# Other block borders for the routing, a limit on its steps, and a later tile: local-global attention and a mixture of experts on one core

## The chip, the core and the metric

The kernel runs on one core of one Trainium2 chip. Its time is device time in microseconds (us) of one execution. Of the kernel before three runs were taken, and the median counts. One more execution was recorded by the hardware profiler.

## The reference

Four batches of 8 heads, 768 tokens of 64 values each, go through an attention in which a token sees the 8 first tokens and the last 96 up to itself, with a bias that grows with the distance. The outputs, 3072 tokens of 512 values, go through a layer of 8 experts, of which each token takes the two with the highest noisy logits. Cut to its core:

```python
scores = scale * np.matmul(q, k.transpose(0, 1, 3, 2)) - slopes * dist      # kept where global or local
a = np.exp(scores - max); a = a / (sum(a) + 1e-9)
x = (a @ v).transpose(0, 2, 1, 3).reshape(3072, 512)

logits = x @ w_gate                                        # 3072 x 8
noisy = logits + np.log1p(np.exp(x @ w_noise)) * noise
top2 = the two largest of noisy in each row                # expert numbers
w = softmax over these two
for e in range(8):
    for k in range(2):
        m = top2[:, k] == e
        out[m] += w[m, k] * (np.maximum(x[m] @ w1[e], 0) @ w2[e])   # w1: 512x1024, w2: 1024x512
```

## The kernel before

**Tiles and stages.** The tokens are 24 tiles of 128. The first stage, the attention, ends a little after 155 us in the trace (its last L899); expert 0 follows, and then the other seven experts, in an order that the kernel finds itself. All of it is one program with an order written out by hand: each engine does its instructions in the order in which the Python code issues them. Multiplications of float32 data in the experts are made of three of a shorter type each: `cut` (lines 195 to 197) has ScalarE round a tensor to its high part (L196) and VectorE subtract that from it (L197).

**Half blocks.** The attention loop (its body is in `tile_local_global_attention_then_moe`, the `for n in range(0, NPAIR, 2)`) goes over half blocks, two to a tile, four heads each. In one of them come, in this order: `score` for the half block after it (L862 on VectorE, four instructions), `trans` (L878, transposes on TensorE), for the tile before `gate_s` or `gate_t`, `product` for the second next (L848 on TensorE), `norm` for the half block before the last (L910, L912, L915 on VectorE; its result `y` is a tile of x), `attend` (L899 on TensorE), `gate_s` or `gate_l`, and `finish`. So a tile's attention and its gate (`gate_t`: transposes; `gate_l`: logits, L410; `gate_s`: a selector product, L423 or L426) lie some half blocks apart. The gate products are made for two tiles at once; `partner` says which go together, and the last tile of a block with an odd number of tiles (`ALONE`) has one for itself, L410, with its transposed tile in `ys[2]`.

**Routing.** The tiles fall into five blocks (`SEG`), of 6, 6, 5, 4 and 3 tiles. When the last tile of a block has its logits, a generator `route(r)` does the block's routing: the noise's softplus (L472 to L497), the two largest (`max` L502, `max_index` L504), positions of the tokens in their expert by TensorE (L552, L554), and then per tile a `mask` (L579), a `marks` (L603, 128 x 336 values on VectorE) and, per up to three tiles (all in the third block), a table sum on TensorE (L628) that L632 adds to a table `tab` of token numbers and weights. The table thus tells for each expert and place which token stands there. Only one block at a time may be in its marks (`marking`). Block 2 (`CLOSE`), the third, closes the tokens from which expert 0's first 512 are taken: it gathers them at once, from the copy `xe` that `gate_l` stores of every tile up to the block's end (`xe<-y` in the trace). Blocks 3 and 4 give the rest.

A generator does its next step when the loop calls it: `tick(place)` after each of the four scores and each of the three steps of a norm lets one active generator do one step, and `finish` lets each do up to 5 (3 for the first two blocks) more. A generator that waits for another engine says so and is passed over until a later place.

**Expert 0 and what runs beside it.** The first four tiles of tokens are transposed (`turn`), and then `up(0, f)` for f = 0 to 7 makes 12 matmuls of 512 columns each (L1132), evicted by `evict` (ScalarE L1113, VectorE L1117). After each third matmul `ahead()` works off one of 32 slots of a table `slots`: it takes the fourth block's generator (`late`) or the fifth's (`last`) up to a step whose number stands there. When all 96 are done `rank()` orders the experts by their counts (from L290 on VectorE), and GpSimd gathers expert 0's last 300 tokens, while TensorE does `down` (L1169). `whole_words` (L236, GpSimd copies) puts their words together, `turn` (L347, in banks named `sc` too) transposes them, and the second half of expert 0's first layer (`up(1, f)`) and of its second (`second(0)`) follow. While `second(0)` runs, `prepare(1)` lists what makes expert 1's operands ready: `weights` (cuts of w1's blocks, `w1_`) and `tokens` (four parts a tile: sums, L1319 to L1322, and three cuts; `z` is the last tile, of 22 tokens a half). The first product of expert 1 is L1426, in a bank named `bank`. From there on the order is the same in both kernels.

The two lists that the change and the prediction speak of most:

```python
SEG = [(0, 6), (6, 12), (12, 17), (17, 21), (21, NT)]              # line 66
...
x, y, z = (tokens(1, t) for t in range(1, 4))
return [*pair[2:], x[0], *join[4:6], w1_[0], *x[1:3], join[6], x[3], *held[:2], y[0], held[2], *y[1:3],
        *w1_[1:], y[3], *z[:3], *get[:2], z[3]]                    # prepare(1), line 1345
```

## Time and profile before

| | us |
|---|---|
| runs | 697.83, 699.15, 701.33 |
| median | 699.15 |
| profiled execution, its own time | 698.98 |
| span of its instructions | 697.3 |
| mean granted TensorE clock | 0.998 |

The profile's page gives the busy time of each engine over the span. Two of its lines matter beside those shown further down: the memory system moved 116.61 MB at a mean of 167 GB/s, and the granted clock of TensorE stood at 9 (90% or more) in each of the 40 slices of the span. A row of the timeline stands for one or more instructions of one line in direct succession: its start, the time from the start of the first to the end of the last, engine, line, operation, output and inputs by the program's names with their shapes, the count, and in brackets, where the engine was idle just before, for how long and what it had waited for. The end of a matmul is modelled, so that rows of TensorE overlap; its starts are measured.

### The profile page before, as it was taken

The numbers are of one execution on the slowest core, as the hardware profiler recorded it, in microseconds if no ns is written. First come the engines' busy times: TensorE is split into PE (matmuls) and PEld (weight loads), VectorE is DVE, ScalarE is ACT, GpSimd is POOL, SyncE is SP. The second block draws the span as 40 slices with busy tenths as digits, with TensorE's granted clock in tenths as the row PEclk, the third lists the DMA queues.
The fourth block names the chain that finished last, engine by engine and source line by source line (L and its number), as shares of the span: only waits on it lengthen the run. The fifth ranks groups of instructions, "written<-read, shape, count | busy, mean of one in ns | idle before, by whom it ended". The sixth has DMA issues, their size and how long they took to land. (4 is left out here: it accounts for less than half of the span.)

```text
span 697.3 us, 16022 instructions
## 1 busy us (share of the span) xinstructions
PE 682.5 (98%) x5701; PEld 615.8 (88%) x5701; DVE 460.2 (66%) x1412; ACT 424.3 (61%) x912; POOL 325.6 (47%) x408
## 2 busy tenths in 40 slices
PE   7999999999999999999999999999999999999995
PEld 5888888888889899999999998999998899889984
DVE  6668788968938478557846694767367757847500
ACT  6888787762346576557755774585458547745510
POOL 3352738350188672264536445552745344541222
PEclk9999999999999999999999999999999999999999
DMA  8999988859394898267945874695569547943233
GB/s 240 331 300 312 275 250 264 305 181 334 128 273 88 155 199 159 52 120 163 193 69 116 183 157 79 140 189 110 93 151 240 94 107 165 186 72 91 31 47 49
DMA packets 132889, 116.61 MB, mean 167 GB/s; under 512 B 51866, under 2 KB 97050, under 8 KB 132800
## 3 DMA queue, kind: packets, MB, share of 16 engines
q1 hardware_dynamic: 121392, 89.35, 46.8%
q0 software_dynamic: 11264, 25.89, 21.4%
q8 instruction: 47, 0.77, 0.5%
q10 hardware_dynamic: 144, 0.26, 0.2%
q14 instruction: 42, 0.34, 0.1%
HBM read 71.07 MB, written 33.10 MB: 149 GB/s over the span
## 5 line engine op out<-in xcount | busy, mean ns | idle before, releaser
L1426 PE MATMUL bank<-xh,wall 128*128 128x384 f32 (+4 forms) x784 | 216.1, 342 | 0.0
L1426 PEld LDWEIGHTS bank<-xh,wall 128*128 128x128 f32 x784 | 144.1, 188 | 3.2
L1426 PE MATMUL bank<-xl,wall 128*128 128x384 f32 (+4 forms) x392 | 133.5, 341 | 1.4 <-DVE xl L197 1.4
L1145 POOL DMA_INDIRECT out_dram<-y,ids x40 | 65.1, 1628 | 123.8 <-ACT y L1142 120.9
L1169 PE MATMUL av<-w2h,hh 128*128 128x512 f32 x304 | 119.6, 393 | 0.0
L1169 PE MATMUL av<-w2h,hl 128*128 128x512 f32 x304 | 119.1, 392 | 0.0
L1169 PE MATMUL av<-w2l,hh 128*128 128x512 f32 x304 | 119.1, 392 | 0.0
L197 DVE TENSOR_TENSOR wall<-raw,wall 128x512 fp32r<-128x512 f32 (+1 forms) x84 | 76.0, 912 | 52.9 <-ACT wall L196 52.9
L196 ACT ACTIVATE wall<-raw 128x512 fp32r<-128x512 f32 (+1 forms) x84 | 57.9, 699 | 45.6 <-POOL raw L1279 45.5
L1117 DVE SCALAR_TENSOR_TENSOR hl<-bank,hh 128x384 fp32r<-128x384 f32 (+4 forms) x84 | 47.2, 562 | 51.0 <-ACT hh L1113 50.5
L1426 PEld LDWEIGHTS bank<-xl,wall 128*128 128x128 f32 x392 | 73.9, 188 | 4.5 <-DVE xl L197 1.8
L865 ACT ACTIVATE a<-ns,mx 128x168 f32<-128x168 f32 (+1 forms) x192 | 67.9, 423 | 14.6 <-DVE mx L862 14.2
L251 POOL DMA_INDIRECT xg<-xd,ids x49 | 53.1, 1084 | 41.6 <-DVE place L302 29.8
L862 DVE CUSTOM_DVE_ANT_0 ns<-sc,bias 128x168 f32<-128x168 f32 (+1 forms) x188 | 51.9, 321 | 25.0 <-PE sc L848 11.4
L1169 PEld LDWEIGHTS av<-w2h,hl 128*128 128x128 f32 x304 | 57.1, 188 | 12.6
L1169 PEld LDWEIGHTS av<-w2l,hh 128*128 128x128 f32 x304 | 57.1, 188 | 9.3 <-DVE w2l L197 0.3
L1169 PEld LDWEIGHTS av<-w2h,hh 128*128 128x128 f32 x304 | 57.1, 188 | 9.1
L1113 ACT ACTIVATE hh<-bank 128x384 fp32r<-128x384 f32 (+4 forms) x84 | 41.8, 498 | 37.0 <-DVE bank L1500 24.7
L1278 POOL TENSOR_TENSOR raw<-raw 128x256 f32<-128x256 f32 x28 | 22.5, 803 | 81.4 <-DVE wall L197 80.8
L899 PE MATMUL av<-vs,at 128*64 128x65 f32 (+1 forms) x768 | 57.3, 224 | 0.0
L236 POOL COPY xt<-y 128x256 uint16<-128x256 uint16 x96 | 35.1, 403 | 46.4 <-DVE y L915 43.6
L899 PEld LDWEIGHTS av<-vs,at 128*64 128x64 f32 (+1 forms) x768 | 50.8, 136 | 2.4 <-issue 1.8
(219 smaller groups left out, 1466.1 us busy)
## 6 DMA issues: line engine op xcount, KB each, us to landing
raw<-in_w SPq DMA_DIRECT2D x64, 256.0 KB
raw<-in_w SPq DMA_DIRECT2D x32, 512.0 KB
out_dram<-zero SPq DMA_DIRECT2D x14, 512.0 KB
vs<-in_v SPq DMA_DIRECT2D x24, 260.0 KB
xd<-xt SPq DMA_DIRECT2D x24, 256.0 KB
qbuf<-in_q SPq DMA_DIRECT2D x23, 256.0 KB
ks<-in_k SPq DMA_DIRECT2D x20, 272.0 KB
xe<-y SPq DMA_DIRECT2D x17, 256.0 KB
```

Source lines behind the costliest of these rows:

```text
L196: nc.scalar.activation(hi, src, AF.Copy)
L197: eng.tensor_sub(lo, src, hi.bitcast(F32))
L236: nc.gpsimd.tensor_copy(to[:, :, c], frm[:, :, c])
L251: nc.gpsimd.indirect_dma_start(out=xg[e, t].bitcast(U16)[:m], out_offset=None, in_=xd[:n], in_offset=bass.IndirectOffsetOnAxis(ap=r, axis= ...
L862: nc.vector.tensor_tensor_reduce(out=ns[x][:, s, :w], in0=ps[:, s], in1=bias[:, u + x, s] if i else bias0[:, u + x, s], scale=-scale, scal ...
L865: nc.scalar.activation(A[n + x][:, s * w:(s + 1) * w], ns[x][:, s, :w], AF.Exp, bias=mx[x][:, s:s + 1], scale=-1.0)
L899: nc.tensor.matmul(ps[s * Q:(s + 1) * Q, h], a[r:z, part * P + q0:part * P + q0 + Q], t[r:z, c], start=k == 0 and (n == 1 or h == 0), stop ...
L1113: nc.scalar.activation(inner(e)[0][j][:, f, :src.shape[1]], src, AF.Relu)
L1117: nc.vector.scalar_tensor_tensor(lo, src, 0.0, hi.bitcast(F32), op0=OP.max, op1=OP.subtract)
L1145: ins = nc.gpsimd.indirect_dma_start(out=out, out_offset=bass.IndirectOffsetOnAxis(ap=r, axis=0), in_=y, in_offset=None, bounds_check=N + ...
L1169: nc.tensor.matmul(ps, x[j][:, f, cols], w[:, f], start=n == 0, stop=n == 3 * FC - 1)
L1426: nc.tensor.matmul(ps, wb[c % 2][u][:, 2 * a + k], x[v][:, 2 * b + k], start=start and n == 0, stop=stop and n == 5, skip_group_check=True)
```

## The change

- The blocks are 6, 6, 4, 4 and 4 tiles. No tile is alone in its gate product any more; `ys[2]` is not used for it, and the last pair's transposed tiles stand in two tiles of their own (`xg`), where they stood in `pairs[0]`. Tile 16 belongs to the fourth block, so it isn't stored in `xe`.
- A generator's steps in one half block are limited by `PACE`: to 10 when the third block's routing is active, to 6 when the fourth's (or the fifth's) is; the other blocks' have no limit. The count `left` is shared by `tick` and `finish`.
- The addition of 2.0 in the softplus (L476) is made by ScalarE, and the step that stood for it remains only in the last two blocks. The copy of token numbers into `val` goes away, since `val` is one tile for all blocks, into which the numbers are written once at the start.
- The table `slots` is timed anew. Before, `late` was asked for its end in slot 29 and `last` stood at step 52 in slot 31; now `late` is asked for its end in slot 17, and `last` stands at step 63 in slot 31.
- In `prepare(1)`, `w1_[1:]`, the last two cuts of weights, move from before `y[3]` (the third tile's last cut) to the list's end; the parts of the last tile `z` and two gathers for the expert after it (`get`) stand in another order.

```diff
-    SEG = [(0, 6), (6, 12), (12, 17), (17, 21), (21, NT)]
+    SEG = [(0, 6), (6, 12), (12, 16), (16, 20), (20, NT)]
...
-    tok = consts.tile([P, NT, 2], F32, name="tok")
+    vals = small.tile([P, NT, 2, 3], F32, name="val")
...
-            if j == 0:
-                XT[g + 1] = pairs[0].rearrange("p (k j t) -> p k j t", k=KC, j=2)
-            to = XT[g + 1 - j][:, :, j]
+            if j == 0 and g == NT - 2:
+                XT[g + 1] = [gp.tile([P, Dm], F32, name="xg", bufs=7).rearrange("p (k t) -> p k t", k=KC) for _ in "ab"]
+            elif j == 0:
+                x = pairs[0].rearrange("p (k j t) -> p k j t", k=KC, j=2)
+                XT[g + 1] = [x[:, :, i] for i in range(2)]
+            to = XT[g + 1 - j][j]
...
         nc.scalar.activation(u, u, AF.Exp, scale=-1.0)
+        nc.scalar.activation(t, u, AF.Copy, bias=2.0)
         yield True
-        nc.vector.tensor_scalar(t, u, 2.0, None, op0=OP.add)
-        yield
+        if r > CLOSE:
+            yield
         nc.vector.reciprocal(t, t)
...
-        val = small.tile([P, SW, 2, 3], F32, name="val")[:, :w]
+        val = vals[:, a:z]
...
-            nc.vector.tensor_copy(val[:, :, :, 0], tok[:, a:z])
...
+        PACE = (99,99,10,6,6)
+        left = [0]
+
         def begin():
+            left[0] = min([PACE[r] for _, r in active], default=99)
...
         def go(y):
             x = y[0]
+            left[0] -= 1
...
-                if y[0].ready <= place:
+                if y[0].ready <= place and left[0] > 0:
                     return go(y)
...
-                while n and y in active and y[0].ready <= END:
+                while n and y in active and y[0].ready <= END and left[0] > 0:
...
-            28: [(last, 48)], 29: [(late, 99), split], 30: [split], 31: [(last, 52)],
+            28: [(last, 57)], 29: [split], 30: [(last, 61), split], 31: [(last, 63)],
...
-                        *w1_[1:], y[3], *z[:3], *get[:2], z[3]]
+                        get[0], y[3], *z[:2], get[1], z[3], z[2], *w1_[1:]]
```

Three places show how instructions move. In the lists an instruction stands with its line, operation, output and inputs, with the elements of one partition behind the 128; "x2" is two in succession. Lines of the changed kernel are 3 to 8 higher than those of the one before.

**VectorE, the norm behind the tile of y whose place a store still reads**, at 115.50 us in the trace (the tile is written by L915, in the change L923). L502 and L504 (L506 and L508) are the third block's two largest, L603 (L606) the marks of the second block, L862 (L870) the scores. Before:

```order
L915 TENSOR_TENSOR y_98<-av,den 128x256
L502 MAX aside<-aside 128x8
L504 MAX_INDEX aside<-aside 128x8
L502 MAX aside<-aside 128x8
L504 MAX_INDEX aside<-aside 128x8
L502 MAX aside<-aside 128x8
L504 MAX_INDEX aside<-aside 128x8
L502 MAX aside<-aside 128x8
L504 MAX_INDEX aside<-aside 128x8 x2
L508 TENSOR_TENSOR aside<-aside 128x5
L510 CAST ixf_3042<-aside 128x10
```

and after the change:

```order
L923 TENSOR_TENSOR y_98<-av,den 128x256
L506 MAX aside<-aside 128x8
L508 MAX_INDEX aside<-aside 128x8
L606 TENSOR_TENSOR xg<-aside 128x336 x2
L870 ISA ns,mx<-sc,bias 128x168
L870 ISA mx 128x1
L506 MAX aside<-aside 128x8
L508 MAX_INDEX aside<-aside 128x8
L870 ISA ns,mx<-sc,bias 128x168
L870 ISA mx 128x1
L506 MAX aside<-aside 128x8
L508 MAX_INDEX aside<-aside 128x8
```

What came in one row behind such a norm is now spread between the scores of the next half block, and the second block's marks, which were past by then, stand ahead of these scores.

**TensorE, the end of the up products of expert 0** (L1132, in the change L1140; `at` and `sc` are the banks of the seventh and the eighth product, `lg` that of the table sums, L628 and L631). Before:

```order
L628 MATMUL lg<-xg,wall 128x168 x2
L1132 MATMUL at<-wall,xh 128x512 x2
L1132 MATMUL at<-wall,xl 128x512
L1132 MATMUL sc<-wall,xh 128x512 x2
L1132 MATMUL sc<-wall,xl 128x512
...
L1132 MATMUL sc<-wall,xh 128x512 x2
L1132 MATMUL sc<-wall,xl 128x512
L628 MATMUL lg<-xg,wall 128x168 x6
```

and after:

```order
L631 MATMUL lg<-xg,wall 128x168 x6
L1140 MATMUL at<-wall,xh 128x512 x2
L1140 MATMUL at<-wall,xl 128x512
L1140 MATMUL sc<-wall,xh 128x512 x2
L1140 MATMUL sc<-wall,xl 128x512
...
L1140 MATMUL sc<-wall,xh 128x512 x2
L1140 MATMUL sc<-wall,xl 128x512
L631 MATMUL lg<-xg,wall 128x168 x2
L1140 MATMUL sc<-wall,xh 128x512 x2
L1140 MATMUL sc<-wall,xl 128x512
```

The first row before is the fourth block's last sum. The sum over the three tiles of the last block (six matmuls) stood behind the eighth product; now the sum over its first three tiles stands fifteen matmuls before that product's end, and the one over its fourth tile nine matmuls behind the seventh product.

**VectorE, ahead of the first product of expert 1.** `xl` and `wall` are the low parts of tokens and weights, 128x44 the sums of the 22-token tile. Before:

```order
L197 TENSOR_TENSOR xl<-xg,xh 128x2x128
L197 TENSOR_TENSOR wall<-raw,wall 128x768
L197 TENSOR_TENSOR wall<-raw,wall 128x512
L197 TENSOR_TENSOR xl<-aside,xh 128x8x128
L1319 TENSOR_TENSOR aside<-xg 128x44
...
L1322 TENSOR_TENSOR aside<-aside,xg 128x44
L197 TENSOR_TENSOR xl<-xg,xh 128x4x22
L197 TENSOR_TENSOR xl<-xg,xh 128x2x22
L197 TENSOR_TENSOR xl<-aside,xh 128x8x22
```

and after:

```order
L197 TENSOR_TENSOR xl<-xg,xh 128x2x128
L197 TENSOR_TENSOR xl<-aside,xh 128x8x128
L1327 TENSOR_TENSOR aside<-xg 128x44
...
L1330 TENSOR_TENSOR aside<-aside,xg 128x44
L197 TENSOR_TENSOR xl<-xg,xh 128x4x22
L197 TENSOR_TENSOR xl<-aside,xh 128x8x22
L197 TENSOR_TENSOR xl<-xg,xh 128x2x22
L197 TENSOR_TENSOR wall<-raw,wall 128x768
L197 TENSOR_TENSOR wall<-raw,wall 128x512
```

The two cuts of weights stood ahead of the last tiles' cuts; now they stand behind all of them.

## Rows read from the trace of the kernel before

**Rows 1.** The page's busy time of each engine, its share of the span, its instructions.

```profile
PE 682.5 (98%) x5701; PEld 615.8 (88%) x5701; DVE 460.2 (66%) x1412; ACT 424.3 (61%) x912; POOL 325.6 (47%) x408
```

**Rows 2.** Busy time by window: length, PE, PEld, DVE, ACT, POOL, clock, DMA share, GB/s.

```profile
120.00:140.00 20.00, 19.96 (x356) 17.56 (x357) 19.27 (x130) 15.06 (x43) 7.61 (x15) 1.00 0.86 303
```

**Rows 3.** Timeline of TensorE, three half blocks (at 117, 141 and 146 us).

```profile
117.14 0.43 PE L410 MATMUL m<-y,wgn 128*32 128x128 f32 x8
117.49 0.66 PE L878 MATMUL at<-ident,a 128*128 128x128 f32 x4
...
118.34 0.97 PE L848 MATMUL sc<-ks,qbuf 64*64 64x168 f32 x16
...
119.24 0.69 PE L899 MATMUL av<-vs,at 128*64 128x65 f32 x16
...
141.57 0.80 PE L848 MATMUL sc<-ks,qbuf 64*64 64x168 f32 x16
142.19 0.22 PE L899 MATMUL av<-vs,at 64*64 64x65 f32 x1
...
146.80 0.27 PE L899 MATMUL av<-vp,at 104*64 104x65 f32 x1 [0.36 <-issue]
```

**Rows 4.** Timeline of VectorE, a norm that waits and the scores behind it.

```profile
115.50 0.42 DVE L915 TENSOR_TENSOR y<-av,den 128x256 f32<-128x256 f32 x1 [0.65 <-DMA xe<-y]
...
117.28 0.32 DVE L862 CUSTOM_DVE_ANT_0 ns<-sc,bias 128x168 f32<-128x168 f32 x1
```

**Rows 5.** Timeline of VectorE, routing steps alone and between scores.

```profile
122.31 0.67 DVE L488 SCALAR_TENSOR_TENSOR aside<-aside 128x40 f32<-128x40 f32 x3
...
123.26 0.33 DVE L862 CUSTOM_DVE_ANT_0 ns<-sc,bias 128x168 f32<-128x168 f32 x1
123.51 0.20 DVE L490 SCALAR_TENSOR_TENSOR aside<-aside 128x40 f32<-128x40 f32 x1
123.62 0.33 DVE L862 CUSTOM_DVE_ANT_0 ns<-sc,bias 128x168 f32<-128x168 f32 x1
```

**Rows 6.** Timeline of TensorE, the last up products of expert 0.

```profile
178.07 0.63 PE L1132 MATMUL sc<-wall,xh 128*128 128x512 f32 x2
...
180.80 0.80 PE L628 MATMUL lg<-xg,wall 128*128 128x168 f32 x6
181.44 0.43 PE L1169 MATMUL av<-w2h,hh 128*128 128x512 f32 x1
```

**Rows 7.** Timeline of VectorE, the seventh product's eviction and a mark.

```profile
178.90 0.69 DVE L1117 SCALAR_TENSOR_TENSOR hl<-at,hh 128x512 fp32r<-128x512 f32 x1 [0.54 <-ACT hh L1113]
...
179.90 0.50 DVE L603 TENSOR_TENSOR xg<-aside 128x336 fp32r<-128x336 f32 x1
```

**Rows 8.** Timeline: the table's last addition, the ranking's start, GpSimd's copies, the transposes.

```profile
185.97 0.32 DVE L632 TENSOR_TENSOR tab<-tab,lg 128x168 f32<-128x168 f32 x1
...
186.33 0.16 DVE L290 SCALAR_TENSOR_TENSOR ids<-tab,dump 128x3 int32<-128x3 f32 x1
...
193.86 4.73 POOL L236 COPY xt<-xg 128x256 uint16<-128x256 uint16 x12
...
197.59 1.31 PE L347 MATMUL sc<-ident,xt 44*128 44x44 f32 x4
```

**Rows 9.** Timeline ahead of expert 1's first product: ScalarE, VectorE, TensorE.

```profile
227.14 1.07 ACT L196 ACTIVATE xh<-aside 128x1024 fp32r<-128x1024 f32 x1 [1.79 <-DVE aside L1322]
...
227.62 1.55 DVE L197 TENSOR_TENSOR wall<-raw,wall 128x768 fp32r<-128x768 f32 x2
...
229.09 1.22 DVE L197 TENSOR_TENSOR xl<-aside,xh 128x1024 fp32r<-128x1024 f32 x1
...
230.35 0.20 DVE L1319 TENSOR_TENSOR aside<-xg 128x44 f32<-128x44 f32 x1
...
231.06 0.36 DVE L197 TENSOR_TENSOR xl<-xg,xh 128x88 fp32r<-128x88 f32 x2
...
231.35 0.45 PE L1426 MATMUL bank<-xl,wall 128*128 128x406 f32 x1 [1.39 <-DVE xl L197]
```

More of the change, by code (lines that the diff above doesn't have):

```diff
@@ L405, in gate_l @@
         x = XT.pop(g)
-        x = [x] if j is None else [x[:, :, i] for i in range(2)]
+        x = [x] if j is None else x
         for i, y in enumerate(x):
@@ L767, in route_consts @@
                            allow_small_or_imprecise_dtypes=True)
-            nc.gpsimd.iota(tok, pattern=[[P, NT], [0, 2]], base=DUMP, channel_multiplier=1,
+            nc.gpsimd.iota(vals[:, :, :, 0], pattern=[[P, NT], [0, 2]], base=DUMP, channel_multiplier=1,
                            allow_small_or_imprecise_dtypes=True)
@@ L1219, in tile_local_global_attention_then_moe @@
         slots = {
[L1220 to L1227 removed]
+            0: [(late, 33)], 1: [(late, 35)], 2: [(gate_t, 1), (late, 37)], 3: [(late, 39)],
+            4: [(gate_l, 1), (late, 42)], 5: [(late, 45)], 6: [(gate_s, 1), (late, 48)], 7: [(last, 2)],
+            8: [(late, 52), (last, 5)], 9: [(last, 8)], 10: [(late, 54), (last, 10)], 11: [(last, 13)],
+            12: [(late, 57), (last, 15)], 13: [(last, 18)], 14: [(last, 21)], 15: [(late, 61), (last, 23)],
+            16: [(last, 26)], 17: [(late, 99)], 18: [(last, 30)], 19: [(last, 33)],
+            20: [(last, 36)], 21: [(last, 39)], 22: [(last, 42)], 23: [(last, 45)],
+            24: [(last, 48)], 25: [], 26: [(last, 52)], 27: [(last, 54)],
+            28: [(last, 57)], 29: [split], 30: [(last, 61), split], 31: [(last, 63)],
         }
```

7 lines of the change are left out of this document (removed).

## The prediction, made before the changed kernel ran

> **What bounds the kernel now.** I began with the page's table of busy times: TensorE is busy for 682.5 of 697.3 us, 98%; VectorE is at 66%, ScalarE at 61%; but from 120 to 140 us VectorE is busy for 19.27 of 20 [rows 1, 2]. A matmul's length there is modelled, so a wait can hide in it. I therefore read the TensorE timeline row by row, and took the time from the first score product of a half block to the first attention product behind it. Undisturbed it is 142.19 - 141.57 = 0.62 us; in the half block that starts at 117.49 it is 119.24 - 118.34 = 0.90 [rows 3]. The excesses, found so, are small: five half blocks between 117.5 and 138 us lose 0.45 (the one shown, products and attention together), 0.36, 0.39, 0.05 and 0.20 us, 1.5 in all, and the one at 143.96 loses 0.6, of which the 0.36 at 146.80 is the visible part [rows 3]. Behind that there are two more: the transposes of expert 0's last tiles wait for GpSimd's copies (the last group, 44 columns, spans 1.31 us [rows 8]), and expert 1's first product waits 1.39 us for VectorE [rows 9]. From 232 us to the end the order is the same in both kernels. So the most that this change can give back is some 2 + 0.9 + 1.4 us, plus the little TensorE work it removes: about 5 us of 699.
>
> Why do the half blocks lose time? Before the first of them VectorE waits 0.65 us until a store has read a tile of y; then come three table marks, and the next scores start only at 117.28 [rows 4]. That wait is in the changed kernel too: tile 15, whose store holds it up, is still stored. From there to 138 us VectorE has the third block's routing between the scores.
>
> **The price of a routing step.** A step put between two score instructions costs VectorE 123.62 - 123.51 = 0.11 us from start to start; three steps that each depend on the one before cost 0.67, so 0.22 each; a score costs 123.51 - 123.26 = 0.25 [rows 5]. [...]
>
> **The change, part by part.** Times are against the profiled execution, 698.98 us (span 697.3 and 1.7 around it); the median of the runs shown is 0.17 higher.
>
> 1. *TensorE work ahead of expert 0's first product.* Tile 16 no longer has a gate product alone: 117.49 - 117.14 = 0.35 less [rows 3]. The third block's table sum has 8 matmuls for 10, about 0.2 less, and the fourth block's position product moves ahead, about 0.15 more. Sum: -0.4.
>
> 2. *Waits in the half blocks.* The limit of ten steps spreads the third routing over more of them, and it begins one tile (two half blocks) earlier. But it now meets the second block's last marks. I laid the new VectorE rows in order behind the same end of the y wait. After that wait come one table sum, a mark and five dependent steps (1.6 us), so the scores start at 117.4, as now. Then come four scores (1.0), eight steps between other work (0.9), two marks (0.4 to 0.5 each [rows 7]) and the norm's own half microsecond: the next scores start at 120.6. TensorE's products wait for the banks that these scores free. It would lose about 1.1 us in the first of these half blocks and 0.85 in the second, and then VectorE has caught up: 1.9 where 1.5 is lost now. The 0.6 us at 143.96 goes, since its half block no longer closes a block; the half block at 137.8 now does, and I leave 0.3 for it. Sum: +0.1, bounds -2.1 (no wait left) and +3.2 (second rival).
>
> 3. *Up products of expert 0.* Between the first and the last of these 96 matmuls TensorE now also does a whole pair's gate product for one tile's (+0.2), one selector product and one position product less (-0.25), and the last table sums, which stood behind them: six matmuls, 181.44 - 180.80 = 0.64, and one pair more, 0.2 [rows 6]. Their sum to the end of the up products: +0.8.
>
> 4. *New waits among them.* The last block's fourth mark stands on VectorE behind the seventh eviction, and its table sum on TensorE only nine matmuls after that product. By the present rows the seventh product's last matmul is followed at 178.07 by the next; its eviction starts on VectorE at 178.90, then comes the mask, and the mark, from 179.90, ends at 180.40: 2.33 after 178.07 [rows 6, 7]. Twelve matmuls take 180.80 - 178.07 = 2.73, nine 2.05. In the present order the sum stands twelve matmuls behind and finds the mark ready; nine behind, it waits 0.3. The three-tile sum before it moves in the same way behind the sixth eviction, and VectorE is in arrears by then (the fourth routing's eighteen steps fill it from 167 us on): 0.35. Sum: +0.65; bounds 0 and 1.5.
>
> 5. *Ranking.* The last addition to the table stands ahead of the last weight cuts and no longer between them and the ranking: 186.33 - 185.97 = 0.36 less [rows 8]. Items 1 to 5 put the ranking at -0.4 + 0.1 + 0.8 + 0.65 - 0.36 = +0.8 us. What follows is a chain without slack: gathers and copies fill GpSimd up to 198.59 (193.86 + 4.73), and TensorE's transposes at 197.59 wait for the last of them [rows 8]. So the 0.8 us goes straight to TensorE.
>
> 6. *Expert 1's last tile.* Now VectorE cuts two weight blocks (229.09 - 227.62 = 1.47) ahead of the third tile's last cut and the 22-token tile [rows 9]. Without them it waits for ScalarE, whose cut of the same tile starts at 227.14 and takes 1.07: to 228.25. Then come the cut, 1.26 to the next start, the four sums, 0.71, and the first cut [rows 9]: the product goes on at 230.5 for 231.35. Gain 0.84; bounds 0 and 1.4. The weight cuts, now behind, end at about 232.7, before the addition that closes VectorE's queue there; they are wanted only for the second chunk, about 9 us later.
>
> 7. *Fewer VectorE steps.* Five additions of 2.0 go to ScalarE and five copies go away, 0.1 to 0.2 us each by the prices above. They are left out of the steps counted in items 2 and 4 and give nothing besides, since the others lie beside TensorE work that does not wait; on ScalarE they fall into its idle 39% [rows 1].
>
> Sum: 0.8 - 0.84 = 0. **Forecast: no change, 699.1 us**, its own range 697.6 to 700.8.
>
> **Rivals.**
> *The waits in the half blocks vanish* because ten steps a half block leave VectorE time to spare. For it: it is only 66% busy. Against it: the y wait stays. Then item 2 is -2.1 and, with no arrears, item 4 is 0: items 1 to 5 give -0.4 - 2.1 + 0.8 - 0.36 = -2.06, with item 6 -2.9: 696.2. Chance 0.16.
> *VectorE cannot carry the third routing* (slower). If a step costs its 0.20 instead of 0.11, the 42 or so steps that are interleaved in the five half blocks from 111 us on cost 42 x 0.09 = 3.8 us more; VectorE is idle for 0.7 of 20 us there [rows 2] and can take no more than that, so TensorE waits some 3.2 more: 702.3. It decides once more than five steps of a half block cost their full length. For it: these steps are a chain. Against it: [rows 5]. Chance 0.12. [...]
> *The moved tile gains nothing*: the weight cuts covered VectorE's wait for ScalarE, and ScalarE's own cut of these weights, now behind the tile, delays the copies that follow. Then item 6 is 0 and the ranking's 0.8 stays: 700.0. Chance 0.17.
>
> **How the numbers follow.** The forecast has 0.55. A measurement of this kernel tells 0.5%, 3.5 us, from no change. The range 696.2 to 701.6 holds the forecast and the third rival, and leaves out about half of the first and three quarters of the second, 0.17. Faster by over 3.5 us needs nearly all waits to go: 0.05. Slower by as much needs the second rival at its full price: 0.06. The same: 0.89.
>
> **What would show it.** In the changed profile: the scores of the half block near 117 us start no earlier than now and the next two half blocks carry the largest TensorE waits (item 2); TensorE waits some 0.3 us at each of the last two table sums (item 4); VectorE's first ranking instruction comes 0.8 us later than 186.33 (items 1 to 5); expert 1's first product waits 0.5 to 0.8 us, not 1.39 (item 6). I am wrong in item 2 if the ranking starts before 185.5 us, and in item 6 if that wait is gone, or as long as now.

## The result and the profile after

| | before | changed |
|---|---|---|
| runs (us) | 697.83 to 701.33 | 704.45 to 706.74 |
| median of 6 runs each | 698.92 | 705.59 |
| ratio, 95% interval | | 1.0089, 1.0071 to 1.0107 |
| profiled execution, span | 698.98, 697.3 | 705.18, 703.4 |

The change makes the kernel 0.9% slower, 6.7 us; the forecast was no change, and 705.59 lies above its range. Cut at instructions that both kernels have, the two profiled executions differ so:

| stretch | before | changed | difference | forecast |
|---|---|---|---|---|
| start to expert 0's first up product | 155.96 | 160.42 | +4.46 | -0.3 (items 1, 2) |
| its up products, first to last | 24.84 | 27.52 | +2.68 | +1.45 (items 3, 4) |
| from there to the ranking | 5.53 | 5.05 | -0.48 | -0.36 (item 5) |
| ranking to the first matmul of expert 1's first product | 43.30 | 43.20 | -0.10 | 0 |
| from there to that product's next matmul, which waits | 1.72 | 0.69 | -1.03 | -0.84 (item 6) |
| the rest | 465.95 | 466.52 | +0.57 | 0 |

The sum is +6.1 us. (The up products end at 180.80 and 187.94, where other work follows on TensorE; the ranking starts at 186.33 and 192.99.) The last +0.57 was not taken apart. The busy times (the page's table, the changed kernel) tell nearly nothing, as TensorE does almost the same work:

```profile
PE 684.3 (97%) x5699; PEld 615.2 (87%) x5699; DVE 460.6 (65%) x1405; ACT 424.2 (60%) x916; POOL 322.4 (46%) x406
```

The window of [rows 2] tells more (same columns). TensorE is busy for 18.56 us instead of 19.96, and VectorE, which was full, for 17.30:

```profile
120.00:140.00 20.00, 18.56 (x331) 15.61 (x324) 17.30 (x105) 13.33 (x37) 7.11 (x15) 1.00 0.88 294
```

**Behind the wait for y.** VectorE's timeline, the place of [rows 4]. The wait for the store that reads a tile of y is now 1.38 us, not 0.65. The scores start at 118.05, the next ones at 121.75, where I had said 117.4 and 120.6:

```profile
115.97 0.42 DVE L923 TENSOR_TENSOR y<-av,den 128x256 f32<-128x256 f32 x1 [1.38 <-DMA xe<-y]
...
118.05 0.32 DVE L870 CUSTOM_DVE_ANT_0 ns<-sc,bias 128x168 f32<-128x168 f32 x1
...
120.51 1.31 DVE L606 TENSOR_TENSOR xg<-aside 128x336 fp32r<-128x336 f32 x2
121.75 0.32 DVE L870 CUSTOM_DVE_ANT_0 ns<-sc,bias 128x168 f32<-128x168 f32 x1
```

The length of this wait alone is not what costs. In e13, the same kernel once more, it lasts 0.83 us and the scores start at 117.43, as forecast; but the next ones start at 121.35 (VectorE's timeline of e13), and TensorE loses 3.0 us there, where it loses 3.4 here:

```profile
117.43 0.32 DVE L870 CUSTOM_DVE_ANT_0 ns<-sc,bias 128x168 f32<-128x168 f32 x1
...
121.35 0.32 DVE L870 CUSTOM_DVE_ANT_0 ns<-sc,bias 128x168 f32<-128x168 f32 x1
```

TensorE's timeline of the changed kernel beside it, in two pieces. Each group of sixteen score products is cut in two by waits for a bank that VectorE's scores have not freed (the releaser named is only the VectorE step next to them):

```profile
117.54 0.66 PE L886 MATMUL at<-ident,a 128*128 128x128 f32 x4
118.88 0.47 PE L856 MATMUL sc<-ks,qbuf 64*64 64x168 f32 x2 [0.69 <-DVE aside L494]
119.59 0.79 PE L856 MATMUL sc<-ks,qbuf 64*64 64x168 f32 x14 [0.24 <-DVE aside L498]
...
122.63 0.47 PE L856 MATMUL sc<-ks,qbuf 64*64 64x168 f32 x2 [0.39 <-PE m L380]
123.52 0.79 PE L856 MATMUL sc<-ks,qbuf 64*64 64x168 f32 x14 [0.42 <-DVE aside L512]
```

From 113.66 to 125.14, 11.48 us, TensorE does work that takes 8.05 at the start-to-start spacing which the same groups have where nothing waits: it loses 3.4. The half blocks at 130.52 and 135.62 lose 0.38 and 0.5 more.

**At the gathers.** Behind a block's last gate product (L413) ScalarE copies the result (L416), and TensorE multiplies that (L426). Here is GpSimd's timeline in that stretch, the first and the last of the four gathers of expert 0's tokens:

```profile
139.37 1.30 POOL L244 DMA_INDIRECT xg<-xe,ids  x1 [2.98 <-PE sc L856]
...
143.59 0.99 POOL L244 DMA_INDIRECT xg<-xe,ids  x1 [0.30 <-issue]
```

The two between start at 140.97 and 142.29, each 0.3 us behind the one before it. Then ScalarE's, the copy here and the one behind the next gate product (154.02):

```profile
142.99 0.28 ACT L416 ACTIVATE aside<-m 128x128 f32<-128x128 f32 x1 [3.31 <-PE at L886]
...
154.73 0.28 ACT L416 ACTIVATE aside<-m 128x128 f32<-128x128 f32 x1 [0.76 <-PE m L413]
```

and TensorE's:

```profile
140.10 0.64 PE L413 MATMUL m<-pair,wgn 128*32 128x128 f32 x16
140.68 0.87 PE L886 MATMUL at<-ident,a 128*128 128x128 f32 x6
143.32 0.41 PE L426 MATMUL lg<-sel,aside 128*128 128x32 f32 x2 [1.77 <-ACT aside L416]
```

The gate product was through at about 140.74. ScalarE, idle and waiting for nothing else, hears of it at 142.99, 2.2 us later; the copies behind the gate products before and after it (125.14 and 154.02) start 0.06 to 0.07 us behind the product's end. TensorE loses 2.4 us here.

The trace of before has such a late signal too, beside the same four gathers. There ScalarE's copy is in time (144.09), but VectorE's scores are late. The score products start at 144.91 us before and at 144.92 in e16, which is the kernel before without the gathers; the scores behind them start 1.1 us apart (VectorE's timelines of before and of e16):

```profile
147.01 0.33 DVE L862 CUSTOM_DVE_ANT_0 ns<-sc,bias 128x168 f32<-128x168 f32 x1 [2.19 <-PE sc L848]
```

```profile
145.88 0.33 DVE L860 CUSTOM_DVE_ANT_0 ns<-sc,bias 128x168 f32<-128x168 f32 x1 [1.42 <-PE sc L846]
```

From that gate product to the next TensorE takes 12.00 us before and 11.40 in e16: these are the 0.6 us that I had put down to the closing of a block (item 2).

**Among the up products.** TensorE's timeline, with the places of [rows 6]:

```profile
174.05 0.46 PE L631 MATMUL lg<-xg,wall 128*128 128x168 f32 x2 [0.27 <-DVE aside L500]
...
177.35 0.18 PE L555 MATMUL lg<-aside,upper 128*128 128x32 bf16 x1 [0.73 <-DVE tab L635]
...
186.92 0.46 PE L631 MATMUL lg<-xg,wall 128*128 128x168 f32 x2
187.94 0.39 PE L1177 MATMUL av<-w2h,hh 128*128 128x512 f32 x1
```

Start to start, TensorE loses 0.43 at 174.05, 0.89 at 177.35, 0.16 at a sum at 183.02 and 0.31 at 186.92: 1.8 us, where I had 0.65. At 174.05 the row names a step of the last block (L500), which reads the bank `lg` until 174.00; the mark that the sum needs had ended at 173.23. The largest loss comes from VectorE's queue too. TensorE waits for the table's addition (L635); this stands on VectorE behind the last block's routing steps and an eviction (L1125), and VectorE has no pause there (its timeline):

```profile
175.83 0.18 DVE L533 RECIPROCAL we<-aside 128x4 f32<-128x4 f32 x1
175.92 0.66 DVE L1125 SCALAR_TENSOR_TENSOR hl<-sc,hh 128x512 fp32r<-128x512 f32 x1
...
176.98 0.32 DVE L635 TENSOR_TENSOR tab<-tab,lg 128x168 f32<-128x168 f32 x1
```

ScalarE's half of the eviction (L1121) is late too, as its timeline shows:

```profile
175.12 0.21 ACT L518 ACTIVATE aside<-aside 128x4 f32<-128x4 f32 x1 [3.42 <-DVE aside L512]
175.23 0.58 ACT L1121 ACTIVATE hh<-sc 128x512 fp32r<-128x512 f32 x1
```

A routing step of the last block (L518) stands on ScalarE ahead of it and waits for VectorE. The product was through at about 173.78 (its last matmul starts at 173.39), so the half comes some 1.4 us late; the 3.42 are ScalarE's whole idle time. But it is done at 175.81, before VectorE reaches its own half, so it does not set this wait.

**Expert 1's first product**, the place of [rows 9]: 0.35 us of wait instead of 1.39 (TensorE's timeline).

```profile
236.88 0.45 PE L1434 MATMUL bank<-xl,wall 128*128 128x406 f32 x1 [0.35 <-DVE xl L197]
```

### The profile page after: what moved, and what is told of

It reads as the page before. It is cut to its first block, busy times and chain, and to the rows that moved or that the text cites. A ratio compares the mean times of both kernels' runs of the same rounds, so it can differ in the third digit from the quotient of the medians.

```text
span 703.4 us, 16004 instructions
## 1 busy us (share of the span) xinstructions
PE 684.3 (97%) x5699; PEld 615.2 (87%) x5699; DVE 460.6 (65%) x1405; ACT 424.2 (60%) x916; POOL 322.4 (46%) x406
## 4 chain that ended last, share of the span: by engine, by line
PE 79%; DVE 6%; issue 6%; ACT 3%; POOL 2%; DMA 2%; POOLq 0%; DVEq 0%; ACTq 0%
PE bank L1434 28%; PE av L1177 22%; PE av L1200 7%; PE av L907 6%; PE at L886 4%; PE sc L856 4%; PE at L1140 2%; POOL out_dram L1153 1%; PE m L380 1%; PE sc L1140 1%; PE bank L1223 1%; PE m L413 1%; DMA xe<-y 1%; DVE xl L197 1%; DMA out_dram<-zero,ids 1%
## 5 line engine op out<-in xcount | busy, mean ns | idle before, releaser
L1153 POOL DMA_INDIRECT out_dram<-y,ids x40 | 65.1, 1626 | 123.5 <-ACT y L1150 120.6
L1125 DVE SCALAR_TENSOR_TENSOR hl<-bank,hh 128x384 fp32r<-128x384 f32 (+4 forms) x84 | 47.1, 561 | 51.7 <-ACT hh L1121 51.2
L870 DVE CUSTOM_DVE_ANT_0 ns<-sc,bias 128x168 f32<-128x168 f32 (+1 forms) x188 | 52.2, 320 | 25.6 <-PE sc L856 9.3
L1121 ACT ACTIVATE hh<-bank 128x384 fp32r<-128x384 f32 (+4 forms) x84 | 41.8, 498 | 37.3 <-DVE bank L1508 25.0
```

The source lines that it names most:

```text
L870: nc.vector.tensor_tensor_reduce(out=ns[x][:, s, :w], in0=ps[:, s], in1=bias[:, u + x, s] if i else bias0[:, u + x, s], scale=-scale, scal ...
L1121: nc.scalar.activation(inner(e)[0][j][:, f, :src.shape[1]], src, AF.Relu)
L1125: nc.vector.scalar_tensor_tensor(lo, src, 0.0, hi.bitcast(F32), op0=OP.max, op1=OP.subtract)
L1153: ins = nc.gpsimd.indirect_dma_start(out=out, out_offset=bass.IndirectOffsetOnAxis(ap=r, axis=0), in_=y, in_offset=None, bounds_check=N + ...
```

## The experiments

Every kernel was timed beside the kernel before on the same chip, and its ratio is to that; a ratio is followed by its 95% interval. "Loss" is time that TensorE loses in the profiled execution of the kernel named. At the gathers it is the time from the gate product (L413) near 140 us (143 with the old blocks) to the next one, above that of the same work without gathers: 11.54 us in e15, 11.40 in e16.

### Which part of the change costs

**e1: the kernel before with the new order of `prepare(1)` alone.**

```diff
-                        *w1_[1:], y[3], *z[:3], *get[:2], z[3]]
+                        get[0], y[3], *z[:2], get[1], z[3], z[2], *w1_[1:]]
```

> The kernel before with the new order of expert 1's preparation alone (the last two cuts of weights go to the end of the list). Theory: the wait of 1.39 us ahead of expert 1's first product falls to some 0.3 us, as in the changed kernel, and nothing else moves: 1.0 us faster than before, 697.9. Rival (the weights come late for the second chunk of expert 1, or ScalarE's copies do): the wait comes back within the next 15 us and the time is that of before, 698.9.

Measured: 697.84, ratio 0.9987 (0.9976 to 0.9997). The wait is 0.50 us (TensorE's timeline):

```profile
230.76 0.45 PE L1426 MATMUL bank<-xl,wall 128*128 128x406 f32 x1 [0.50 <-DVE xl L197]
```

Item 6 holds. (The wait itself varies: 0.92 to 1.89 us with the old order in the recorded executions of before, e7, e16 and e17, 0.75 or less with the new order.)

**e5: the changed kernel with the blocks, and the table `slots`, of before.**

```diff
-    SEG = [(0, 6), (6, 12), (12, 16), (16, 20), (20, NT)]
+    SEG = [(0, 6), (6, 12), (12, 17), (17, 21), (21, NT)]
```

> The changed kernel with the blocks of before (6, 6, 5, 4, 3) and the old table of slots; the limits on steps, the additions on ScalarE, the tile for the token numbers and the new preparation of expert 1 stay. Theory (the new blocks cost the time: the third routing meets the second one's marks, the gathers meet the fourth block's close, and the last two routings meet in the up products): the time is that of the new preparation alone or a little less, 697.0 to 698.5. Rival (the limits, or the work moved to ScalarE, have a part in it): 700 to 704.

Measured: 697.11, ratio 0.9983 (0.9974 to 0.9993). The new blocks, with the timing in `slots` that goes with them, carry the whole loss; what is left of the change is a small gain. This version is the fastest of the three by a little.

**e11: e5 without limits on the steps.**

```diff
-        PACE = (99,99,10,6,6)
+        PACE = (99,99,99,99,99)
```

> The kernel with the old blocks and slots and the rest of the change (697.1 us), without its limits on steps (all 99). Theory (with the old blocks the routings do not meet, so the limits hardly bind and the work taken off VectorE gives the little that was gained): within 0.5 us of 697.1. Rival (the limits spread the steps there too and give the 0.7 us that this kernel is faster than the new preparation alone): 697.8 to 698.3.

Measured: 698.56, ratio 0.9982 (0.9967 to 0.9997), as e5, though this execution has late signals at the gathers and that of e5 has none. With the old blocks the limits do nothing that can be measured.

**e4: the same edit on the changed kernel.**

> The changed kernel without its limits on steps in a half block (all 99). Theory (the second and the third routing meet because the third block ends a tile earlier; the limits push some of it on): the steps pile up in one half block; TensorE's losses between 114 and 126 us, 3.4 us, stay within 0.7 us of that, and the gathers still follow one another: 705 to 706.3. Rival (the limits cause the loss, since they keep the second block's marks back until the next scores): the losses between 114 and 126 us fall to the 1.5 of the kernel before, and the time by about 2 us, to 703.6.

Measured: 714.21, ratio 1.021 (1.0186 to 1.0234), worse than either theory had it. With the new blocks the limits are needed. TensorE waits 1.57 us at 119.47 and 1.89 at 123.48 (its timeline), and in the window behind that its granted clock is at the lower level for most of the time (0.57 is the mean over the 8 us):

```profile
123.48 0.18 PE L555 MATMUL lg<-aside,upper 128*128 128x32 bf16 x1 [1.89 <-DVE aside L524]
```

```profile
122.00:130.00 8.00, 6.52 (x68) 5.13 (x68) 3.67 (x27) 3.24 (x9) 0.83 (x3) 0.57 0.67 233
```

The clock is at that level for some 17 us between 122 and 157, so at half the speed up to 8.5 of this kernel's 15 us more are the clock's (an estimate: TensorE works for most of these 17 us, but not all).

### The half blocks behind the wait for y

**e2: y in a third buffer**, so that no norm waits for a store.

```diff
-                XR[g] = ys[g % 2].rearrange("p (h d) -> p h d", h=H)
+                XR[g] = ys[g % 3].rearrange("p (h d) -> p h d", h=H)
```

> The changed kernel, with three tiles of y in turn where it had two, so that a norm no longer waits for the store of the tile two before. Theory (the norm's wait of 1.38 us before 115.97 us is what puts VectorE in arrears ahead of the third routing): the scores that start at 118.05 start some 1.2 us earlier, TensorE's losses between 114 and 126 us (3.4 us) fall below 1.5, and the time falls by about 2 us, to 703.5. Rival (VectorE has too many steps there whether it waited or not): the scores of the next half block, at 121.75, move by under 0.5 us and the time by under 0.7.

Measured: 704.78, ratio 1.0078 (1.0056 to 1.0099). The wait is gone, and the loss from 114 to 126 us is 2.5, not 3.4: 0.9 of the 2 us that my theory gave it. The larger part is VectorE's arrears. In this execution the gathers lost 4.35 (the granted clock is 0.50 from 144.3 to 147.6 us, behind them), so the time alone would have misled.

**e8 and e9: the third routing limited to 7 and to 9 steps a half block.**

```diff
-        PACE = (99,99,10,6,6)
+        PACE = (99,99,7,6,6)
```

> The changed kernel with a limit of 7 steps instead of 10 while the third block's routing is active. Theory (VectorE is in arrears from 115 to 126 us because ten steps and a score take more than a half block of TensorE): fewer steps per half block leave it time: TensorE's losses between 114 and 126 us fall from 3.4 to under 2, and as the routing ends later the gathers come two half blocks later, past the fourth block's close: 701.5 to 703.5. Rival (the marks of 0.5 to 0.65 us each, not the number of steps, make the arrears): the losses stay, and the later end of the third block pushes steps into the fourth's: 705 to 708.

> The changed kernel with a limit of 9 steps instead of 10 while the third block's routing is active. With 7 the losses between 114 and 126 us nearly went, but the gathers came so late that the first transposes waited 3.1 us for them. Theory (the number of steps per half block is what VectorE cannot carry, and the place of the gathers costs the rest): TensorE's losses between 114 and 126 us are 2 to 2.6 us, the gathers come after the fourth block's close or one half block before the transposes need them, without the 3.1 us: 701.5 to 703.5. Rival (10 against 9 makes no difference to VectorE; the gain with 7 was where the second block's last marks fell): 704.5 to 706.

Measured: with 7, 700.75, ratio 1.0039 (1.002 to 1.0057); with 9, 701.71, ratio 1.003 (1.0015 to 1.0045). With 7 the loss from 114 to 126 us falls to 0.8, so the arrears come from the routing steps, the second block's marks among them. Which of the two weighs more is not shown: with 7 the last two marks also move, behind the scores of the next two half blocks (to 123.36 and 124.03). But the block ends later, and so do its gathers; the transposes of the gathered tiles now wait for them (e8, TensorE's timeline):

```profile
152.83 0.66 PE L347 MATMUL sc<-ident,xg 128*128 128x128 f32 x4 [0.42 <-DMA xg<-xe,ids]
155.00 1.01 PE L347 MATMUL sc<-ident,xg 128*128 128x128 f32 x4 [1.51 <-DMA xg<-xe,ids]
```

From the gate product at 148.18 to the first up product this takes 9.89 us, 3.6 more than in e18 (6.26): some 2.3 are these two waits, and the rest is the clock, whose mean is 0.52 from 155 to 158.5 us. With 9 the marks stay where they were, the loss from 114 to 126 us is still 2.3, but those at 130 and 135 us are gone. None of the limits tried (7, 9, 10) clears both: the arrears go only as the gathers come late.

### The up products

**e10: the fourth block's steps asked for earlier in `slots`** (its end in slot 11, no longer 17), and the gathers two places later, as in e6.

```diff
-            16: [(last, 26)], 17: [(late, 99)], 18: [(last, 30)], 19: [(last, 33)],
+            10: [(late, 61), (last, 10)], 11: [(late, 99), (last, 13)],
...
+            16: [(last, 26)], 17: [], 18: [(last, 30)], 19: [(last, 33)],
```

> The kernel with the gathers two half blocks later (702.06 us), and a table of slots in which the fourth block's marks and its end come earlier (its first three marks before the first eviction, its end in slot 11 instead of 17). Theory (in the up products TensorE waits 0.4 us for the fourth block's last mark and 0.9 us for its last addition to the table, both late because the fifth block's steps stand ahead of them on VectorE): both waits go, the up products take 26.2 to 26.6 us instead of 27.5, and the time is 700.7 to 701.2. Rival (VectorE has too much to do in the up products in any order): the waits move to the last sums and the time stays at 702.1.

Measured: 704.58, ratio 1.0068 (1.0044 to 1.0093). The up products take 1.44 us less than in e6, which shares the rest of the program with it (26.37 for 27.81), and neither the fourth block's last sum nor the position product waits any more (TensorE's timeline):

```profile
171.58 0.35 PE L631 MATMUL lg<-xg,wall 128*128 128x168 f32 x2
...
177.29 0.19 PE L555 MATMUL lg<-aside,upper 128*128 128x32 bf16 x1
```

The 1.44 us are there; a loss of 3.9 at the gathers, where e6 had none, hid them. Here too the clock is at 0.50 behind the gathers, from 147.9 to 151.3 us.

**e12: the three mends together**, a limit of 9, three buffers for y and e10's `slots`, without the later gathers.

> The changed kernel with a limit of 9 steps, three tiles of y in turn, and the table of slots with the fourth block's end in slot 11. Theory (the three losses are separate and add up): against the change (705.6), some 0.9 us less at the wait for y, 1 to 1.5 less by the limit, 2 less at the gathers, 1.1 less in the up products: 699.5 to 701. Rival (the losses are one: VectorE is late and a mend at one place shows as a wait at the next): over 702.

Measured: 699.62, ratio 1.0003 (0.999 to 1.0016); up products 26.10 us, loss at the gathers 1.1. The time is what the sum of the mends gave, and the new blocks, mended, come back to the time of before, no further. Of the sum, the 1.3 us less at the gathers is not shown to be a mend's doing.

### The gathers

In both programs the gathers come in pairs; a generator's `yield LAST` behind one lets other work onto GpSimd. On GpSimd itself copies stand between the second and the third gather before the change (from 142.45 to 143.87 us), but not in the changed kernel, where all four follow one another.

**e3: a `yield LAST` behind each gather, which brings a copy between the second and the third again. e7: the kernel before with all four in a row. e6: the changed kernel with the gathers two places later.**

```diff
-                if t % 2:
-                    yield LAST
+                yield LAST
```

```diff
-                if t % 2:
+                if t == TA - 1:
                     yield LAST
```

```diff
+            yield LAST
+            yield LAST
             for t in range(TA):
                 gather(0, t)
```

> The changed kernel, with one of the four gathers of expert 0's tokens in each half block, where two pairs came in successive half blocks and follow one another on GpSimd with nothing between. Theory (gathers in a row hold back the signal that a TensorE instruction is done): the 2.2 us between the gate product's last matmul at 140.47 us and ScalarE's copy of it at 142.99 fall to 0.3 to 1.0, TensorE's loss of 2.4 us there falls to 0.6 or less, and the time is 1.5 to 2 us shorter, 703.7 to 704.1. Rival (TensorE's late signal comes from something else at this place, the loading of its instructions for one): the 2.2 us stay, and the time is that of the change, 705.6.

> The kernel before with its four gathers in a row on GpSimd, where two pairs have the copies of a tile between them. Theory (as for the gathers two half blocks later): the third and fourth gather now run from 142.7 to 145 us, over the fourth block's close (the logits' last matmul at 143.75, the selector product at 144.67), so TensorE loses 1.5 to 2.5 us there instead of 0.6: 700 to 701. Rival (the gathers alone do not hold up the signals; the changed kernel's crowded VectorE is needed for it): within 0.4 us of the kernel before, 698.9.

> The changed kernel with its four gathers two half blocks later, still one after the other on GpSimd. Theory (what costs is not that they follow one another but where they fall: TensorE's signals come late while they are issued, and at the fourth block's close TensorE waits for ScalarE's answer to such a signal, the logits' copy): behind that close nothing waits so closely, TensorE loses 0.3 to 1.0 us there and not 2.4, and the time is 1.4 to 2 us shorter, 703.6 to 704.2. Rival (four in a row cost their 2.4 wherever they fall): the loss moves along with them and the time stays at 705.6.

Measured: e3 704.82, ratio 1.009 (1.0067 to 1.0112), and the loss stays at 2.3: such a copy does not take it away. e7 698.49, ratio 1.0007 (0.9997 to 1.0018): no late signal at all, against my 700 to 701. e6 702.06, ratio 1.0056 (1.0039 to 1.0073): no late signal, and no loss at the gathers.

It looked as if the place of the gathers decided. But e5 to e8 were measured together, and none of the four shows a late signal. So I repeated.

**e13: the changed kernel again. e14: e6 again.**

> The changed kernel once more, beside the next three on one chip, since TensorE's signals came late during the gathers in some recorded executions and not in others of the same program (3.9 us lost with the new slots, none with the gathers late, and both are the same instructions up to there). Theory (where the gathers fall decides): as before, 705.6, some 3 us over the kernel with late gathers in this same call. Rival (whether the signals come late changes from one execution to the next, wherever the gathers stand): the two differ by less than 1 us here.

> The changed kernel with the gathers two half blocks later, once more. Theory (the place decides): 702 to 702.8, little spread. Rival (chance from execution to execution): runs of 702 beside runs of 704 to 706, a median within 1 us of the change in this call.

Measured: e13 708.07, ratio 1.0089 (1.0064 to 1.0113), loss at the gathers 4.4; e14 705.82, ratio 1.0062 (1.0034 to 1.0089), loss 5.5, with the very instructions that lost nothing in e6. That theory falls. In e14 TensorE's own matmuls stop without a wait that the profile shows (its timeline), and then its clock is at the lower level (the window):

```profile
147.35 0.21 PE L909 MATMUL av<-vp,at 40*64 40x65 f32 x1 [0.37 <-issue]
...
148.12 0.34 PE L909 MATMUL av<-vp,at 40*64 40x65 f32 x1 [0.43 <-issue]
```

```profile
149.50:154.50 5.00, 5.00 (x61) 4.18 (x58) 2.52 (x19) 3.27 (x9) 0.74 (x2) 0.50 0.30 110
```

**e15 and e16: the changed kernel and the one before without gathers.** Four plain loads bring other rows instead, so expert 0's first four tiles are computed for other tokens.

```diff
-            nc.gpsimd.indirect_dma_start(
-                out=xw[e, t], out_offset=None, in_=xe[:n],
-                in_offset=bass.IndirectOffsetOnAxis(ap=ids0[:, t:t + 1], axis=0), bounds_check=n - 1, oob_is_err=False)
+            nc.sync.dma_start(xw[e, t], xe[DUMP + t * P:DUMP + (t + 1) * P])
```

> The changed kernel, with the four gathers of expert 0's first tokens replaced by four plain loads of the first four tiles on SyncE's queue (so expert 0's first four tiles are computed for other tokens than the table names). Theory (the gathers on GpSimd hold up TensorE's signals): no signal is over 0.6 us late between 136 and 150 us, the 2.4 us there are gone, and the time is 703.0 to 703.6 with little spread. Rival (something else there does it): the loss stays, 705 to 706.

> The kernel before with the same four plain loads for the gathers. Theory: its own loss at the gathers, 0.6 us in the recorded execution and up to 3 in the slowest runs, goes: 697.5 to 698.3, with a spread of 1 us instead of 3. Rival: no difference, 698.9.

Measured, beside e13: e15 703.08, ratio 1.0037 (1.0017 to 1.0057); e16 698.41, ratio 0.9981 (0.9958 to 1.0005). By the medians the gathers cost the changed kernel 708.07 - 703.08 = 5.0 us there; by the ratios it is 0.52% or 3.6 us (e13's ratio sets it beside 701.8 us of the kernel before, whose median there was 699.01). For the kernel before it is 0.6 by the medians, which is not told from none (the interval reaches to 0.42%, 2.9 us). The spread that I had expected to go there stayed: two of the ten runs of e16 took 701.0, with a mean clock of 0.994 and 0.995 where the others had 0.997 to 0.999. Without the gathers ScalarE's copy starts as the gate product ends (e15; ScalarE's timeline, then TensorE's):

```profile
140.75 0.28 ACT L414 ACTIVATE aside<-m 128x128 f32<-128x128 f32 x1 [1.13 <-PE m L411]
```

```profile
141.32 0.31 PE L424 MATMUL lg<-sel,aside 128*128 128x32 f32 x2
```

**e17 and e18: e7 and e3 again, together.**

> The kernel before with its four gathers in a row, once more: in the call where it was timed, no recorded kernel showed late signals at all, so it told nothing. Theory (where signals come late, four gathers in a row cost more than two pairs with copies between: recorded losses 2.4 to 5 us against 0.6 to 2.3): if its profile shows signals over 0.9 us late, it loses 2 to 5 us between 138 and 150 us and its median is 1.5 to 4 us over the kernel before in this call. Rival (pairs or a row make no difference; the changed kernel loses more since its VectorE leaves TensorE less slack): within 1 us of the kernel before, with late signals in its profile.

> The changed kernel with its gathers in two pairs, once more, in the same call. Theory (a row costs more than pairs): 6 us over the kernel before in this call, where the change itself was 6.7 and 9.1 over it, and a loss of at most 2.5 us between 136 and 150 us in its profile. Rival (no difference): 7 to 9 us over it, with a loss of 3 to 5.

Measured: e17 698.58, ratio 0.9993 (0.9975 to 1.0011); e18 702.04, ratio 1.0045 (1.0027 to 1.0062). No late signal in either; in e18 ScalarE's copy behind the gate product of 140.56 starts in time (its timeline):

```profile
141.27 0.28 ACT L416 ACTIVATE aside<-m 128x128 f32<-128x128 f32 x1 [1.13 <-PE m L413]
```

e18 is the kernel of e3, at 1.009 there. So the late signals come or stay away by occasion, not by program, and the spacing of the gathers could not be told apart. Nor is it the chip alone: e5 to e8 and e9 to e12 ran on the same one in two sessions, the first without late signals, the second with them. Where they stay away, the new blocks still cost 0.45%, 3.5 us.

e17 showed one thing more. Its profiled execution took 701.96, the highest of its runs. Expert 1's first product waited 1.89 us (it has the old order of `prepare(1)`), and the granted clock then fell; 0.57 is the mean over this window, and the kernel before, whose wait was 1.39, has 1.00 there (TensorE's timeline of e17, its window, the same window of the kernel before):

```profile
232.77 0.45 PE L1426 MATMUL bank<-xl,wall 128*128 128x406 f32 x1 [1.89 <-DVE xl L197]
```

```profile
234.00:238.00 4.00, 4.00 (x14) 3.39 (x13) 0.59 (x1) 0.51 (x1) 0.23 (x1) 0.57 0.74 231
```

```profile
234.00:238.00 4.00, 4.00 (x26) 3.44 (x25) 0.35 (x1) 1.79 (x3) 1.52 (x1) 1.00 0.42 156
```

## Why the prediction was wrong

**Item 2 is the step that failed**: "+0.1, bounds -2.1 and +3.2". I had 2.2 us of waits in the changed kernel against 2.1 before; there are 3.4 + 0.38 + 0.5 + 2.4 = 6.7, so +4.6 and not +0.1, beyond the upper bound too. It failed in two ways.

*The arrears behind the wait for y were mis-sized.* Mechanism and place were right: the second block's marks and the third routing's steps meet behind that wait, and the next two half blocks carry 3.4 of the 6.7. But I laid the new steps "behind the same end of the y wait", and it ends 0.47 us later; a third buffer takes 0.9 us away (e2). That later end is the smaller part: in e13 the first scores come as forecast, and 3.0 us are lost still, for the 1.9 that I had. I took 0.4 to 0.5 for a mark, and the two took 0.65 each beside a GpSimd copy. The Trainium skill, page "SBUF — State Buffer", section "Who interferes with whom", says that a VectorE instruction with two inputs in that memory and a GpSimd instruction that reads there exclude each other; the trace agrees in kind, as both grew (the mark from 0.5 [rows 7] to 0.65, two copies from 0.73 at 117.69 us to 1.02 at 120.44). It doesn't show a full exclusion: the two marks and the two copies take 1.38 us together, and one after the other they would take 1.73. And I had VectorE caught up after two half blocks, while two more lose 0.9 together. A limit of 7 steps, which leaves 0.8 of the 3.4, shows that the steps, marks included, make the arrears.

*The gathers were not in the sum at all.* The 0.6 us at 143.96 I explained by the block's close from one row, whose releaser was "issue", and wrote that it would go. It came with the gathers (without them, in e16, it is gone), and with the new blocks they lie beside a gate product with a tight chain over ScalarE behind it. There the same late signals cost 2.4 us in this profile, and 3.6 to 5.0 in the pair e13 and e15. The sign that I had named for item 2, a ranking before 185.5 us, looked only the other way: it starts at 192.99, 6.7 later than before where I had 0.8.

Why the same gathers cost the kernel before so much less is only argued: with five tiles in the third block they fall on other work, which waits less on TensorE's signals.

**Items 1 and 3** can be seen only in sums. The measured waits ahead of the up products are 6.7 - 2.1 = 4.6 more, item 1 gives -0.4, and the stretch grew by 4.46: 0.3 is not accounted for. The up products without their waits are longer by 2.68 - 1.8 = 0.9, for +0.8 in item 3.

**Item 4** was of the right kind and too small, 1.8 for 0.65, outside its bound of 1.5. The wait of 0.3 at the fourth mark's sum is there (0.31). At the three-tile sum it is 0.16, not 0.35. The other two I had not looked for: the fourth block's last sum (0.43) and the fifth's position product (0.89). I followed VectorE's queue at the last two sums alone; at these two places, too, TensorE waits for its end: for a step of the last block, and for an addition behind such steps and an eviction. e10 removes both by asking for the fourth block earlier.

**Item 5** was right: -0.48 for -0.36.

**Item 6** was right: -1.03 for -0.84, alone in e1 as well; that the sizes lie so close is partly luck, as the wait differs by up to 1 us between executions with the same order. **Item 7** shows nowhere by itself; e5, which has it with item 6, is as fast as e1 within the intervals.

**The rivals.** "VectorE cannot carry the third routing" had the right sign and place and the wrong mechanism: it wanted a step to cost 0.20 us between scores, and the step at 118.31 and the score behind it at 118.41 stand 0.10 apart, as in [rows 5]. The marks, the longer wait and the sheer number of steps did it. "The waits vanish" was refuted, and so was "the moved tile gains nothing". The range was too narrow since it gave a stretch with a wait that I had not explained by its releaser no chance to grow.

What stays open: why GpSimd's gathers delay TensorE's signals in some sessions and not in others, on the same chip too, and whether the spacing of the gathers matters where they do.

## What to carry to other kernels

A wait of which the profile says only "issue" is not a small constant: look at what the other engines and the DMA queues issue at that moment before you write that it will go. When a planner moves routing or bookkeeping steps, follow every in-order queue they pass through to each product that waits for it: here one table addition behind other routing steps and an eviction held TensorE up for 0.9 us. And test the parts apart, and more than once: here the new blocks cost 7 us in one session and 3.5 in another (e18), while what remained of the change (e5) gained 0.17%.

## What the runs showed of the hardware that I had not expected

- While GpSimd issues its four gathers, 1.0 to 1.3 us each, engines that wait for TensorE hear of it late in some executions (ScalarE's L416 2.2 us after the gate product in the changed kernel, 1.6 in e3 and 3.1 in e2 and e13, but 0.07 in e6, e15 and e18), and now and then matmuls stop for 0.2 to 0.4 us at a time with no wait shown (e14). The loss at the gathers was 0.6 in the profile of before, 0.65 and 0.9 in e11 and e1, and 0 in e5, e7 and e17, all with the old blocks; with the new blocks 1.1 (e12) to 5.5 (e14), or 0 in e6 and e18. In the largest (e2, e10, e13 and e14) a part of it is the granted clock, at 0.50 behind the gathers.
- Behind waits or stops of TensorE its granted clock went from 1.00 to 0.50, from 2.4 to 1.2 GHz, for 3.4 us in e2, e8, e10, e13 and e17 and 6.8 in e14. In e13, with one wait of 2.59 us, this is the window of the wait and the one behind it:

```profile
140.00:144.00 4.00, 1.41 (x24) 0.97 (x12) 0.77 (x3) 0.55 (x3) 3.09 (x4) 1.00 0.55 147
144.00:148.00 4.00, 4.00 (x55) 3.69 (x55) 1.83 (x12) 3.62 (x13) 1.65 (x5) 0.57 0.37 115
```

So a wait can cost more than its own length: the same wait at expert 1's first product left the clock at 1.00 when it lasted 1.39 us (before) and was followed by 0.5 for 3.4 us when it lasted 1.89 (e17). The length of one wait does not decide it: behind the 1.77 us at 143.32 the changed kernel's clock stayed at 1.00, and behind the 1.51 at 155.00 that of e8, which had waited 0.42 shortly before, fell.
